# Softmax row factors of an attention stage: another instruction for the row sums, and Pool for two of the products

## The chip, the core and the metric

The program runs on one core of a Trainium2 chip. Five engines each work through their own queue in the order in which the program was written: TensorE (PE in the profile, with its weight loads as PEld), VectorE (DVE), ScalarE (ACT), GpSimd (POOL) and SyncE (SP), which here starts the DMA transfers. They meet at semaphores. The metric is the time of one execution in microseconds (us) on the device; lower is better.

## The reference

Three layers stand one behind the other. The change lies in the first, an attention over 2 batches, 8 heads, 576 tokens and head size 64; what the two expert layers behind it compute is only named here.

```python
scores = scale * np.matmul(q_rot, k_rot.transpose(0, 1, 3, 2))
scores = scores - np.max(scores, axis=-1, keepdims=True)
attn = np.exp(scores)
attn = attn / (np.sum(attn, axis=-1, keepdims=True) + 1e-09)
attn_out = np.matmul(attn, v)
...
x = _moe_ref(x=x, **moe_kwargs)             # 4 experts, all of them for every token
return _moe2_ref(x=x, **moe2_kwargs)        # 8 experts, one for each token
```

## The kernel before

**Tiles.** The 16 heads are worked off as 8 pairs. For pair `i` the scores of 2 x 576 rows are made in nine chunks of 128 rows by 576 columns: chunks 0 to 3 are rows of the first head, 5 to 8 of the second, and chunk 4 holds the last 64 rows of both. All products keep single precision by splitting each operand into a high and a low part (`..._hi` on one engine, the difference `..._lo` on another).

**One pair.** `load` brings q and k by DMA, `rope` turns them (three operations over 1152 columns, on Pool for nearly all pairs), `split_hi` (ACT) and `split_lo` (L187, Pool) write the parts to tile `n`, of which there is one, and `spread` (L224) copies `n` by ten DMAs of SP's queue to the operands `ka`, `kb`, `qa`, `qb`. Then for each chunk PE makes the scores (`qk`, L327, tile `sc`, a ring of two), DVE takes the negated row maximum (`row_max`, L337, tile `nm`), and ACT the exponential with its row sum (`exp`, L344), which lands in a column of tile `sum`. PE turns the exponentials round (`pt`, L382 to L389), ACT and DVE split them (`pt_hi` L407, `pt_lo` L411), PE multiplies by v (`av`, L424), ACT and DVE bring the halves together in `t` (L432, L438).

**The row factors.** When all nine chunks of a pair have their sums, DVE adds 1e-9 (`row_sum`, L350, `rs`), takes the reciprocal (`row_factor`, L354), and spreads it in two ways: `rest_factor` (L359) multiplies the block mask `blk` (128 x 128) by the factor of chunk 4 and gives `mrs`, and `wide_factor` (L365) repeats the other eight factors 64 times each and gives `rb` (128 x 512). The table `ENG` has `wide_factor` on Pool for seven pairs and on DVE for pair 1. A round later `rmat` on PE turns `rb` round with four transposes (L444) and multiplies `mrs` by `id2`, two identities above each other (L446); `x_norm` (DVE, L455) multiplies `t` by the result, and `x_hi`, `x_lo` write the input of the next layer.

**What sets the order.** `plan` hands every operation to a list scheduler with a rank (`POS`, a table of numbers), an engine, a planned cost and the operations it depends on. The scheduler (`Schedule.run`) plays the plan through and writes the instructions in the order that comes out. On the chip each engine then keeps to that order and waits wherever it comes too early. So `rmat`, `x_norm` and the products by v of pair `i` lie between the scores of pair `i+1`.

**Memory.** The tiles of the pairs' inputs lie in pools on the right side of the SBUF, among them `at_qf`. When the last scores are made, these are closed and the weights of the first expert (`load1`, L648, units `raw0` to `raw3`) are loaded over them. In the first expert layer PE multiplies without a gap (L784 to L786, then L800 to L802).

Of the kernel before, what the change touches and what calls it, by code (L numbers as in the profile page):

```python
# [10 lines left out]
F32 = mybir.dt.float32  # L11
# [84 lines left out]
class Attention:  # L96
# [40 lines left out]
    }  # L137

    ENG = {("rope", 0): "gggggggg", ("rope", 1): "gggggggg", ("rope", 2): "vvgggggg", ("split", 0): "aaaaaaaa",
           ("split", 1): "gggggggg", ("v", 0): "aaagaaaa", ("v", 1): "gggggggg", ("wide", 0): "gvgggggg",  # L140
           ("x", 0): "aaaagggg", ("x", 1): "gggggggg", ("rope1q", 0): "ggv", ("rope1k", 0): "vvv",
           ("split1", 0): "avav", ("first", 0): "vvgvvvvgvgvvgvvg", ("w_lo", 0): "gggv"}
    ENGINES = {"a": "ACT", "v": "DVE", "g": "POOL"}
# [1 line left out]
    def __init__(self, tc, ctx, tails, cst, qk, v, cs, xh, xl):  # L145
        self.tc, self.nc, self.cst = tc, tc.nc, cst
        self.qk_d, self.v_d, self.xh, self.xl = qk, v, xh, xl
        pool = lambda n, b, **k: ctx.enter_context(tc.tile_pool(name=n, bufs=b, **k))
        self.p_x = tails.enter_context(tc.tile_pool(name="at_x", bufs=2))
        self.p_vs = pool("at_vs", 3)  # L150
        self.p_e = pool("at_e", 13)
        self.p_sm = pool("at_sm", 2)
        self.early = ExitStack()
        pool_r = lambda n, b: self.early.enter_context(tc.tile_pool(name=n, bufs=b, side="right"))
        self.p_raw = pool_r("at_raw", 2)
        self.p_n = pool_r("at_n", 1)
        self.p_k = pool_r("at_k", 2)
        self.ps_sc = pool("ps_sc", 2, space=PSUM)
        self.first = ExitStack()
        self.ps_first = self.first.enter_context(tc.tile_pool(name="ps_first", bufs=2, space=PSUM))  # L160
        self.ps_pt, self.pool = None, pool
        nc = self.nc
        fixed = pool("at_fix", 1)
        self.pth = fixed.tile([128, 2, 4, S], F32R, name="pth")
        self.ptl = fixed.tile([128, 2, 4, S], F32R, name="ptl")
        self.p4 = fixed.tile([128, 2, S], F32R, name="p4")
        fixed = pool_r("at_qf", 1)
        self.rope_t, self.cs_d = fixed.tile([128, 2, 2, S], F32, name="cos_sin"), cs
        self.qa = [fixed.tile([128, 640], F32R, name=f"qa{j}") for j in range(2)]
        self.qb = [fixed.tile([128, 640], F32R, name=f"qb{j}") for j in range(2)]  # L170
        for j in range(2):
            nc.vector.memset(self.qa[j][:, S:640].bitcast(F32), 0.0)
            nc.vector.memset(self.qb[j][:, 512:S].bitcast(F32), 0.0)
        self.st = [dict() for _ in range(NPAIR)]

    def by(self, eng):
# [155 lines left out]
    def row_max(self, i, c):  # L332
        nc, st = self.nc, self.st[i]
        if "nm" not in st:
            st["nm"] = self.p_sm.tile([128, 9], F32, name="nm")
            st["sum"] = self.p_sm.tile([128, 9], F32, name="sum")
        nc.vector.tensor_reduce(out=st["nm"][:, c:c + 1], in_=st["sc", c][:, :, :SH],  # L337
                                axis=AX.XY, op=ALU.max, negate=True)

    def exp(self, i, c):  # L340
        nc, st = self.nc, self.st[i]
        e = st["e", c] = self.p_e.tile([128, S], F32, name="e")
        col = 8 if c == 4 else (2 * c if c < 4 else 2 * (c - 5) + 1)
        nc.scalar.activation(out=e.rearrange("p (a b) -> p a b", a=2), in_=st.pop(("sc", c))[:, :, :SH],  # L344
                             func=AF.Exp, bias=st["nm"][:, c:c + 1], accum_out=st["sum"][:, col:col + 1])

    def row_sum(self, i):
        nc, st = self.nc, self.st[i]
        rs = st["rs"] = self.p_sm.tile([128, 9], F32, name="rs")
        nc.vector.tensor_scalar(out=rs, in0=st["sum"], scalar1=1e-9, scalar2=None, op0=ALU.add)  # L350

    def row_factor(self, i):
        rs = self.st[i]["rs"]
# [1 line left out]

    def rest_factor(self, i):
        nc, st = self.nc, self.st[i]
        mrs = st["mrs"] = self.p_sm.tile([128, 128], F32, name="mrs")
        nc.vector.tensor_scalar(out=mrs, in0=self.cst["blk"], scalar1=st["rs"][:, 8:9], scalar2=None, op0=ALU.mult)  # L359

    def wide_factor(self, eng, i):
        st = self.st[i]
        rb = st["rb"] = self.p_sm.tile([128, 8, 64], F32, name="rb")
        sh = [128, 8, 64]
        self.by(eng).tensor_tensor(out=rb, in0=self.cst["one"].unsqueeze(2).to_broadcast(sh),  # L365
                                in1=st["rs"][:, 0:8].unsqueeze(2).to_broadcast(sh), op=ALU.mult)

    def pt(self, i, u):
        nc, st = self.nc, self.st[i]
# [70 lines left out]
    def rmat(self, i):  # L440
        nc, st = self.nc, self.st[i]
        ps = self.ps_sc.tile([128, 2, 512], F32, name="sc").rearrange("p a b -> p (a b)")
        for c in range(4):
            nc.tensor.transpose(ps[:, c * 128:(c + 1) * 128],  # L444
                                st["rb"][:, 2 * c:2 * c + 2].rearrange("p a b -> p (a b)"), self.cst["ident"])
        nc.tensor.matmul(ps[:, 512:S], st["mrs"], self.cst["id2"], start=True, stop=True)  # L446
        st["r"] = ps[:, 0:S]

    def x_parts(self, i):
# [29 lines left out]
    def plan(self, last_round):  # L479
# [15 lines left out]
        for i in range(NPAIR):  # L495
# [36 lines left out]
            for c in range(9):  # L532
# [8 lines left out]
            e = [D["exp", i, c] for c in range(9)]  # L541
            f = op("row_factor", i, 0, "DVE", 9, self.row_sum, i, after=e)
            f = op("row_factor", i, 1, "DVE", 60, self.row_factor, i, after=[f])
            f = [op("row_factor", i, 2, "DVE", 128, self.rest_factor, i, after=[f]),
                 op("row_factor", i, 3, self.letter("wide", 0, i), 400, self.wide_factor, self.letter("wide", 0, i), i,
                    after=[f])]

            def av(p, *keys):
                return [D["av", p, 5 * j + k] for j, k in keys if p >= 0]
# [909 lines left out]
```

## Time and profile before

| | us |
|---|---|
| three timed runs | 791.31, 791.35, 791.45 |
| median | 791.35 |
| the profiled execution | 791.62 |
| its span, first to last instruction | 789.4 |
| mean granted clock of TensorE | 0.993 |

The median and the profiled execution differ by 0.27 us, and 2.22 us of the execution lie outside the span. Over the whole span PE is busy for 94%, DVE for 60%, ACT for 49%, Pool for 18%. The stages differ much: the attention fills the first 184 us, the first expert layer the middle, the routed layer the end.

Times in the rows further down are us from the start of the span. A row of the timeline gives the start, the duration, the engine, the line of the program, the operation with the tiles that it writes and reads, and in square brackets how long the engine had been idle before and what ended that.

### The profile page before, as it was taken

The numbers are of one execution on the slowest core, as the hardware profiler recorded it, in microseconds if no ns is written. First come the engines' busy times: TensorE is split into PE (matmuls) and PEld (weight loads), VectorE is DVE, ScalarE is ACT, GpSimd is POOL, SyncE is SP. The second block draws the span as 40 slices with busy tenths as digits, with TensorE's granted clock in tenths as the row PEclk, the third lists the DMA queues.
The fourth block names the chain that finished last, engine by engine and source line by source line (L and its number), as shares of the span: only waits on it lengthen the run. The fifth ranks groups of instructions, "written<-read, shape, count | busy, mean of one in ns | idle before, by whom it ended". The sixth has DMA issues, their size and how long they took to land. (4 is left out here: it accounts for less than half of the span.)

```text
span 789.4 us, 11018 instructions
## 1 busy us (share of the span) xinstructions
PE 743.1 (94%) x4002; PEld 651.9 (83%) x4002; DVE 471.2 (60%) x876; ACT 390.2 (49%) x793; POOL 145.3 (18%) x118
## 2 busy tenths in 40 slices
PE   1798988899999999999999999999998999999997
PEld 1687877798998999999899899999986678888885
DVE  7988999998222252213522124322367999999993
ACT  4687888786101232111320113211224899999993
POOL 4767785324100000000000000000032001000000
PEclk9899999999999999999999999999999999999999
DMA  5766664615360069910282000000043266594010
GB/s 196 208 167 189 169 167 90 146 65 212 113 199 1 1 208 271 324 51 1 66 265 97 1 1 0 1 1 1 1 187 147 80 236 232 206 365 177 27 42 17
DMA packets 31836, 97.26 MB, mean 123 GB/s; under 512 B 4638, under 2 KB 6174, under 8 KB 25760
## 3 DMA queue, kind: packets, MB, share of 16 engines
q1 hardware_dynamic: 29936, 91.77, 37.2%
q0 software_dynamic: 1840, 4.73, 1.6%
q8 instruction: 33, 0.54, 0.3%
q14 instruction: 27, 0.22, 0.1%
HBM read 58.32 MB, written 27.09 MB: 108 GB/s over the span
## 5 line engine op out<-in xcount | busy, mean ns | idle before, releaser
L790 DVE SCALAR_TENSOR_TENSOR hl<-ps,hh 128x384 fp32r<-128x384 f32 x96 | 53.5, 558 | 269.6 <-ACT hh L789 269.6
L789 ACT ACTIVATE hh<-ps 128x384 fp32r<-128x384 f32 x96 | 47.2, 492 | 304.3 <-PE ps L786 302.7
L654 DVE TENSOR_TENSOR wl<-raw,wh 128x512 fp32r<-128x512 f32 x284 | 178.6, 687 | 7.0 <-ACT wh L653 7.0
L653 ACT ACTIVATE wh<-raw 128x512 fp32r<-128x512 f32 x284 | 156.6, 627 | 4.1 <-SPq L1238 2.5
L784 PE MATMUL ps<-xh,wh 128*128 128x384 f32 x384 | 130.1, 339 | 0.0
L786 PE MATMUL ps<-xh,wl 128*128 128x384 f32 x384 | 129.5, 337 | 0.0
L785 PE MATMUL ps<-xl,wh 128*128 128x384 f32 x384 | 129.3, 337 | 0.0
L800 PE MATMUL acc<-wh,hh 128*128 128x512 f32 x288 | 114.2, 397 | 0.0
L802 PE MATMUL acc<-wh,hl 128*128 128x512 f32 x288 | 114.1, 396 | 0.0
L801 PE MATMUL acc<-wl,hh 128*128 128x512 f32 x288 | 113.5, 394 | 0.0
L785 PEld LDWEIGHTS ps<-xl,wh 128*128 128x128 f32 x384 | 72.1, 188 | 3.9
L784 PEld LDWEIGHTS ps<-xh,wh 128*128 128x128 f32 x384 | 72.1, 188 | 3.9
L786 PEld LDWEIGHTS ps<-xh,wl 128*128 128x128 f32 x384 | 72.0, 188 | 0.0
L901 POOL TENSOR_TENSOR ss<-ss,half 128x1 f32<-128x1 f32 (+1 forms) x5 | 3.5, 705 | 364.3 <-DVE sq L890 364.2
L802 PEld LDWEIGHTS acc<-wh,hl 128*128 128x128 f32 x288 | 54.1, 188 | 12.6
L800 PEld LDWEIGHTS acc<-wh,hh 128*128 128x128 f32 x288 | 54.1, 188 | 9.1 <-issue 0.8
L801 PEld LDWEIGHTS acc<-wl,hh 128*128 128x128 f32 x288 | 54.1, 188 | 8.8
L344 ACT ACTIVATE e<-sc,nm 128x576 f32<-128x576 f32 x72 | 53.4, 743 | 8.6 <-DVE nm L337 8.3
L337 DVE TENSOR_REDUCE nm<-sc 128x1 f32<-128x576 f32 x72 | 53.8, 750 | 3.1 <-PE sc L327 2.0
L389 PE MATMUL pt<-ident,e 128*128 128x128 f32 (+1 forms) x304 | 47.9, 283 | 6.1 <-DVE ptl L411 5.5
L327 PE MATMUL sc<-ka,qa 128*128 128x288 f32 x160 | 33.9, 333 | 17.0 <-POOL qa L187 14.7
L411 DVE TENSOR_TENSOR ptl<-pt,pth 128x512 fp32r<-128x512 f32 x68 | 45.7, 680 | 2.2 <-ACT pth L407 1.4
(231 smaller groups left out, 1240.5 us busy)
## 6 DMA issues: line engine op xcount, KB each, us to landing
raw<-in_w_dram SPq DMA_DIRECT2D x40, 1024.0 KB, 5.8
xs<-z SPq DMA_DIRECT2D x10, 2056.0 KB, 14.1
raw<-in_qk_dram SPq DMA_DIRECT2D x7, 1152.0 KB, 5.4
ka<-n SPq DMA_DIRECT2D x14, 288.0 KB, 3.9
kb<-n SPq DMA_DIRECT2D x14, 288.0 KB, 4.6
xin<-xs SPq DMA_DIRECT2D x13, 257.0 KB, 4.0
rv<-in_v_dram SPq DMA_DIRECT2D x8, 320.0 KB, 5.4
qa<-n SPq DMA_DIRECT2D x14, 144.0 KB, 4.2
```

The source lines that it names most:

```text
L337: nc.vector.tensor_reduce(out=st["nm"][:, c:c + 1], in_=st["sc", c][:, :, :SH], axis=AX.XY, op=ALU.max, negate=True)
L344: nc.scalar.activation(out=e.rearrange("p (a b) -> p a b", a=2), in_=st.pop(("sc", c))[:, :, :SH], func=AF.Exp, bias=st["nm"][:, c:c + 1], ...
L389: nc.tensor.transpose(ps[0:n, c * 128:(c + 1) * 128], st["e", c + 5 * h][:, k * 128:k * 128 + n], ident)
L653: nc.scalar.activation(out=hi, in_=raw, func=AF.Copy)
L654: nc.vector.tensor_tensor(out=lo, in0=raw, in1=hi.bitcast(F32), op=ALU.subtract)
L784: nc.tensor.matmul(o, wcut(self.wh[u], k), xh[:, k, cs], start=(k == 0), stop=False)
L785: nc.tensor.matmul(o, wcut(self.wh[u], k), xl[:, k, cs], start=False, stop=False)
L786: nc.tensor.matmul(o, wcut(self.wl[u], k), xh[:, k, cs], start=False, stop=(k == 3))
L790: nc.vector.scalar_tensor_tensor(out=hl, in0=o, scalar=0.0, in1=hh.bitcast(F32), op0=ALU.max, op1=ALU.subtract)
L800: nc.tensor.matmul(acc, hh[:, js], wh, start=(f == 0), stop=False)
L801: nc.tensor.matmul(acc, hh[:, js], wl, start=False, stop=False)
L802: nc.tensor.matmul(acc, hl[:, js], wh, start=False, stop=(f == 7))
```

## The change

The row sums get a fixed tile for even and one for odd pairs, `sums[i % 2]`, with two columns for every chunk: the sum is written to the first, and the second holds 1e-9 from the start, set once by DVE. `row_sum` adds the two columns with `tensor_reduce` instead of adding a constant with `tensor_scalar`. `rest_factor` multiplies `id2` (128 x 64) by the factor, on Pool instead of DVE, and `rmat` exchanges the operands: `blk` is now the stationary one and `mrs`, half as wide, the moving one. `wide_factor` stands on Pool for all eight pairs. In the plan `rest_factor` gets Pool and 64 columns.

```diff
     ENG = {("rope", 0): "gggggggg", ("rope", 1): "gggggggg", ("rope", 2): "vvgggggg", ("split", 0): "aaaaaaaa",
-           ("split", 1): "gggggggg", ("v", 0): "aaagaaaa", ("v", 1): "gggggggg", ("wide", 0): "gvgggggg",
+           ("split", 1): "gggggggg", ("v", 0): "aaagaaaa", ("v", 1): "gggggggg",
...
+        self.sums = [fixed.tile([128, 9, 2], F32, name=f"sum{j}") for j in range(2)]
+        for t in self.sums:
+            nc.vector.memset(t[:, :, 1], 1e-9)
...
-            st["sum"] = self.p_sm.tile([128, 9], F32, name="sum")
+            st["sum"] = self.sums[i % 2]
...
-                             func=AF.Exp, bias=st["nm"][:, c:c + 1], accum_out=st["sum"][:, col:col + 1])
+                             func=AF.Exp, bias=st["nm"][:, c:c + 1], accum_out=st["sum"][:, col, 0:1])
...
-        nc.vector.tensor_scalar(out=rs, in0=st["sum"], scalar1=1e-9, scalar2=None, op0=ALU.add)
+        nc.vector.tensor_reduce(out=rs, in_=st["sum"], axis=AX.X, op=ALU.add)
...
-        mrs = st["mrs"] = self.p_sm.tile([128, 128], F32, name="mrs")
-        nc.vector.tensor_scalar(out=mrs, in0=self.cst["blk"], scalar1=st["rs"][:, 8:9], scalar2=None, op0=ALU.mult)
-
-    def wide_factor(self, eng, i):
+        mrs = st["mrs"] = self.p_sm.tile([128, 64], F32, name="mrs")
+        nc.gpsimd.tensor_tensor(out=mrs, in0=self.cst["id2"], in1=st["rs"][:, 8:9].to_broadcast([128, 64]),
+                                op=ALU.mult)
+
+    def wide_factor(self, i):
...
-        self.by(eng).tensor_tensor(out=rb, in0=self.cst["one"].unsqueeze(2).to_broadcast(sh),
-                                in1=st["rs"][:, 0:8].unsqueeze(2).to_broadcast(sh), op=ALU.mult)
+        self.nc.gpsimd.tensor_tensor(out=rb, in0=self.cst["one"].unsqueeze(2).to_broadcast(sh),
+                                     in1=st["rs"][:, 0:8].unsqueeze(2).to_broadcast(sh), op=ALU.mult)
...
-        nc.tensor.matmul(ps[:, 512:S], st["mrs"], self.cst["id2"], start=True, stop=True)
+        nc.tensor.matmul(ps[:, 512:S], self.cst["blk"], st["mrs"], start=True, stop=True)
...
-            f = [op("row_factor", i, 2, "DVE", 128, self.rest_factor, i, after=[f]),
-                 op("row_factor", i, 3, self.letter("wide", 0, i), 400, self.wide_factor, self.letter("wide", 0, i), i,
-                    after=[f])]
+            f = [op("row_factor", i, 2, "POOL", 64, self.rest_factor, i, after=[f]),
+                 op("row_factor", i, 3, "POOL", 400, self.wide_factor, i, after=[f])]
```

The order of ACT's and SP's instructions stays as it was; PE's and DVE's changes by one exchange late in pair 7 beside what the diff itself takes out and puts in.

DVE in the middle of a round, about the normalisation of pair 2; before (`nm` is a row maximum, `ptl` and `p_132` low parts of turned exponentials, `t` the output of a pair):

```order
L438 TENSOR_TENSOR t<-av_843,t 64x288
L337 TENSOR_REDUCE nm<-sc 128x1
L411 TENSOR_TENSOR ptl<-pt,pth 128x512 x2
L337 TENSOR_REDUCE nm<-sc 128x1
L359 TENSOR_SCALAR mrs<-blk,rs 128x128
L411 TENSOR_TENSOR ptl<-pt,pth 128x512
L455 TENSOR_TENSOR t<-t,sc 128x576
```

The same place after the change:

```order
L443 TENSOR_TENSOR t<-av_842,t 64x288
L341 TENSOR_REDUCE nm<-sc 128x1
L416 TENSOR_TENSOR ptl<-pt,pth 128x512 x2
L341 TENSOR_REDUCE nm<-sc 128x1
L416 TENSOR_TENSOR ptl<-pt,pth 128x512
L460 TENSOR_TENSOR t<-t,sc 128x576
```

Only the multiplication of `mrs` is gone from DVE's queue.

Pool between the low parts of pair 3 and those of pair 4 (the two rows of `n`); the rows `raw` turn pairs 4 and 5, and `xl` is of pair 0. Before:

```order
L187 TENSOR_TENSOR n<-raw,n 128x1152
L203 TENSOR_TENSOR raw<-raw,cos_sin 128x1152 x2
L187 TENSOR_TENSOR xl<-t,xh 128x576
L205 TENSOR_TENSOR raw<-raw 128x1152
L203 TENSOR_TENSOR raw<-raw,cos_sin 128x1152
L187 TENSOR_TENSOR n<-raw,n 128x1152
```

After:

```order
L191 TENSOR_TENSOR n<-raw,n 128x1152
L370 TENSOR_TENSOR rb<-one,rs 128x512
L207 TENSOR_TENSOR raw<-raw,cos_sin 128x1152
L363 TENSOR_TENSOR mrs<-id_74,rs 128x64
L207 TENSOR_TENSOR raw<-raw,cos_sin 128x1152
L191 TENSOR_TENSOR xl<-t,xh 128x576
L209 TENSOR_TENSOR raw<-raw 128x1152
L207 TENSOR_TENSOR raw<-raw,cos_sin 128x1152
L191 TENSOR_TENSOR n<-raw,n 128x1152
```

`rb` and `mrs` of pair 1 have come in, ahead of the rows that turn pair 4; in the other rounds one `mrs` comes in. Near the end of the attention three first splits of weights (`wl`) have moved ahead of the low parts of pair 6's output (`xl`).

SP's queue where the weights of the first expert are loaded, with the semaphores that each transfer waits for; before:

```order
L765 DMA itau<-in_tau_dram 128x1 [waits DMAHW6_49]
L765 DMA tokid<-in_tokid_dram 128x9 [waits DMAHW7_49]
L648 DMA raw_2067<-in_w_dram 128x2048 [waits DMAHW1_49,DMAHW2_49,DMAHW0_49,PE_49]
L648 DMA raw_2068<-in_w_dram 128x2048
L648 DMA raw_2069<-in_w_dram 128x2048
```

After:

```order
L769 DMA itau<-in_tau_dram 128x1 [waits DMAHW6_49]
L769 DMA tokid<-in_tokid_dram 128x9 [waits DMAHW7_49]
L652 DMA raw_2063<-in_w_dram 128x2048 [waits DMAHW1_49,DMAHW0_49,DMAHW2_49,DVE_49,PE_49]
L652 DMA raw_2064<-in_w_dram 128x2048 [waits DVE_49]
L652 DMA raw_2065<-in_w_dram 128x2048
```

The order is the same, but the fixed sum tiles were put in the pool `at_qf`, over which these weights are loaded: units 1 and 2 now wait for DVE as well, namely for `row_sum` of pair 6 and of pair 7.

## Rows read from the trace of the kernel before

**Rows 1.** Page, the span in 40 slices: busy tenths of DVE

```profile
DVE  7988999998222252213522124322367999999993
```

**Rows 2.** Stretches: length; busy us of PE, PEld, DVE, ACT, Pool; clock, DMA

```profile
64.00:68.00 4.00, 4.00 (x21) 3.88 (x20) 2.36 (x5) 2.12 (x6) 3.01 (x2) 0.57 0.99 213
115.33:135.46 20.13, 17.85 (x129) 15.72 (x128) 19.45 (x30) 16.86 (x38) 12.70 (x7) 1.00 0.42 89
...
157.21:175.52 18.31, 18.13 (x139) 16.95 (x138) 17.11 (x32) 16.11 (x37) 3.13 (x3) 1.00 0.07 20
183.78:789.40 605.62, 593.78 (x2988) 518.32 (x2986) 303.66 (x604) 248.81 (x484) 36.57 (x52) 1.00 0.33 112
```

**Rows 3.** By stage, instructions on rs alone: DVE busy, Pool busy, clock, DMA

```profile
30.00:57.00 27.00, 2.08 (x3) 1.04 (x1) 0.93 0.72 177
57.00:76.00 19.00, 3.23 (x4) 0.00 (x0) 0.91 0.80 232
76.00:94.96 18.96, 2.48 (x3) 1.04 (x1) 1.00 0.60 148
94.96:115.33 20.37, 3.94 (x3) 1.04 (x1) 1.00 0.68 187
115.33:135.46 20.13, 3.70 (x3) 1.04 (x1) 1.00 0.42 89
135.46:156.00 20.54, 3.71 (x3) 1.04 (x1) 1.00 0.59 140
156.00:183.78 27.78, 1.87 (x6) 2.08 (x2) 1.00 0.29 114
```

**Rows 4.** Instructions on tile rs: count, ns shortest/median/longest, first and last start

```profile
L350 DVE TENSOR_SCALAR rs<-sum x8: 164/757/2015, 37.0 to 175.5; 128x9 f32<-128x9 f32 x8
L354 DVE RECIPROCAL rs<-rs x8: 215/216/217, 37.7 to 175.7; 128x9 f32<-128x9 f32 x8
L359 DVE TENSOR_SCALAR mrs<-blk,rs x8: 277/1308/1712, 38.0 to 178.8; 128x128 f32<-128x128 f32 x8
```

**Rows 5.** Timeline of DVE: the row sums of pair 4

```profile
117.27 2.01 DVE L350 TENSOR_SCALAR rs<-sum 128x9 f32<-128x9 f32 x1 [0.23 <-ACT e L344]
```

**Rows 6.** Timeline of Pool: split of pairs 3, 6; turn of pair 5

```profile
58.72 2.65 POOL L187 TENSOR_TENSOR n<-raw,n 128x1152 fp32r<-128x1152 f32 x1 [2.46 <-ACT n L182]
...
76.14 2.68 POOL L203 TENSOR_TENSOR raw<-raw,cos_sin 128x1152 f32<-128x1152 f32 x1 [2.01 <-DMA raw<-in_qk_dram]
...
116.59 2.65 POOL L187 TENSOR_TENSOR n<-raw,n 128x1152 fp32r<-128x1152 f32 x1 [0.41 <-ACT n L182]
```

**Rows 7.** Timeline of SP's queue: start and time of issuing alone

```profile
61.40 1.34 SPq L224 DMA_DIRECT2D ka<-n  x2
...
70.79 0.58 SPq L191 DMA_DIRECT2D raw<-in_qk_dram  x1
...
86.75 4.01 SPq L224 DMA_DIRECT2D qb<-n  x4
...
173.18 31.73 SPq L648 DMA_DIRECT2D raw<-in_w_dram  x7
```

**Rows 8.** Timeline of ACT: split of pair 5, first weight splits

```profile
94.96 1.18 ACT L182 ACTIVATE n<-raw 128x1152 fp32r<-128x1152 f32 x1
...
186.45 2.18 ACT L653 ACTIVATE wh<-raw 128x512 fp32r<-128x512 f32 x4
```

**Rows 9.** Timeline of PE: waits in pairs 0 and 1

```profile
39.90 0.40 PE L424 MATMUL av<-p,vs 128*128 128x288 f32 x1 [1.58 <-DVE p L411]
...
62.58 0.65 PE L389 MATMUL pt<-ident,e 128*128 128x128 f32 x4 [1.18 <-DVE ptl L411]
```

**Rows 10.** DMA issues, 0 to 200 us: KB each, median us to landing

```profile
raw<-in_w_dram SPq DMA_DIRECT2D x7, 1024.0 KB, 5.0
...
qb<-n SPq DMA_DIRECT2D x14, 16.0 KB, 2.0
```

**Rows 11.** Group of Pool by form, 0 to 250 us: busy us, mean ns

```profile
L850 POOL TENSOR_TENSOR scale<-scale,itau 128x8 f32<-128x8 f32 x1 | 0.2, 203 | 0.1
```

## The prediction

> **What bounds the kernel now.** I read the page's slices first, then the stretches, then what the changed instructions cost by stage. The slices [rows 1] show DVE nearly full in the first nine or ten of 40, the attention, and far from full in the middle. From 183.78 us on PE is busy for 593.78 of 605.62 us [rows 2]: the expert layers are PE's, no edited line runs there, and they move as a block with the moment at which the attention ends. So the change is worth what the end of the attention moves.
>
> Inside it one pair takes about 20 us. In the round from 115.33 to 135.46 DVE is busy for 19.45 of 20.13 us, PE for 17.85, ACT for 16.86, Pool for 12.70 [rows 2]. DVE sets the pace, and part of its busy time is no work. `row_sum` handles nine numbers a row and takes between 164 and 2015 ns, `mrs` between 277 and 1712 [rows 4]. In pair 4 `row_sum` starts at 117.27 and ends at 119.28 [rows 5]; Pool's subtraction for `n` started at 116.59 and ends at 119.24 [rows 6]. The nine numbers are held until Pool is through. The reciprocal, on the same engine and operand, takes 215 to 217 ns in all eight pairs [rows 4].
>
> Beside this. The Trainium skill (SBUF — State Buffer, "Who interferes with whom") says why: `tensor_scalar` can use the port pair that VectorE shares with GpSimd and is then blocked for the whole of the other's instruction, while `tensor_reduce` on trn2 never contends. The 2.01 us agree; a `tensor_reduce` from SBUF under a running Pool instruction is in no row here. By that rule the low end below is right; without it the third rival's 8 x 0.6 us would be lost.
>
> **The change part by part.** *What leaves DVE.* Rows 3 give the time of everything that touches `rs`, stage by stage. The stages are cut where ACT begins the high parts of `n` of the next pair, for a reason that follows. What stays of a pair is a row sum and a reciprocal. I take the row sum at 0.16, the shortest it is now, since the new form reads 18 numbers instead of nine; its bounds are that and the present mean of about 1.0 (median 0.76), if the reduction is held in the same way [rows 4]. I take the low end because the reciprocal, also SBUF to SBUF with one tensor input, never varies. With 0.22 for the reciprocal 0.38 stays, and the stages lose: 1.70 (to 57), 2.85 (to 76, with the wide factor of pair 1), 2.10, 3.56, 3.32, 3.33, and 1.11 (two pairs to the end). Together 17.97 us.
>
> *What comes to Pool.* Eight `mrs` of 128x64 and one `rb`. The `rb` costs 1.04 [rows 3]. An `mrs` lies between 0.20, a product of 128x8 [rows 11], and that 1.04; on a straight line between 8 and 512 columns it is an estimate of 0.3. So Pool gets 0.3 us more a round, up to 1.04, and has 7 idle in the round of rows 2. The result is wanted a whole round later (the `mrs` of pair 4 falls due behind 135), in pair 7 a few us later; PE's new wait for it costs nothing, and the `pt` and `av` queued behind it on PE aren't held.
>
> *What is neutral.* On Pool the first weight splits now stand ahead of pair 6's `xl`, which the expert layer reads only from its second block of tokens on, after eight groups of products. The product of `rmat` keeps 64 moving columns and a 128x128 stationary operand. The two fills with 1e-9 fall into DVE's first idle time. The sum column has another stride, which ACT writes as one number a row. On SP units 1 and 2 of the weights get a wait for `row_sum` of pairs 6 and 7. The last row sum starts at 175.5 [rows 4], the loads at 173.18 [rows 7]: unit 2, unit 3 behind it, and the next expert's loads come some 2.5 us later. A load lands 5.0 us after issue [rows 10], so unit 2 is there by about 181.5; ACT's first weight splits of that layer start at 186.45 [rows 8]. That cover is 5 us; without it the cost would be those 2.5.
>
> *How much reaches the end.* Stage by stage:
> - To 57 us: PE waits 1.58 for DVE's `p` of pair 0, right behind its `mrs` [rows 9]. Take 1.6.
> - To 76: with `rb` gone, PE loses its wait of 1.18 for `ptl` [rows 9]. After this gap PE ran from 64 to 68 at a granted clock of 0.57, a mix of the two levels 2.4 and 1.2 GHz [rows 2]; at full clock these 4.00 us would be 2.28. Without the gap I expect no fall: 1.18 + 1.72 = 2.9, about what DVE loses.
> - To 94.96: 2.1. Sum so far 6.6.
> - Here something else is late. Tile `n` exists once, and ACT can write pair 5's high parts at 94.96 [rows 8] only when the ten copies of pair 4 have landed. Going back: the last of them is issued by 90.76 [rows 7], lands 2.0 after an issue of 0.6 [rows 10], thus at 92.2. These copies follow Pool's split of pair 4, which follows the turn that started at 76.14 after waiting for its load [rows 6]; that load was issued at 70.79, behind the ten copies of pair 3 from 61.40 [rows 7], and those behind Pool's split at 58.72 [rows 6]. None of it has DVE in it. The chain moves only with its head, by the 1.6 of the first stage, so ACT can begin at 92.2 - 1.6 = 90.6 at the earliest: 4.4 instead of 6.6. ACT's queue is in order and the pair's last exponentials stand behind; all engines come to wait.
> - To 115.33 and to 135.46: 3.56 and 3.32 on offer. In the stretch from 157.21 to 175.52, in which nothing is held by Pool, PE does 139 instructions in 18.31 us; the 129 of a round would take 17.0 at that rate, 3.1 less than 20.13 [rows 2]. But ACT has 16.86 to do in such a round. I take 85%: 3.0 and 2.8.
> - To 156: ACT has no split of `n` left to do; 90% of 3.33: 3.0.
> - To the end: 80% of 1.11: 0.9.
>
> The sum is 4.4 + 3.0 + 2.8 + 3.0 + 0.9 = 14.1 us. From the profiled execution's 791.62 that gives 777.5. The median of the runs is 0.27 lower, so I forecast **777.3**.
>
> **The rivals.**
> *The loop over n doesn't hold* (copies land earlier, or the head moves more). Then the 6.6 stay, and the later stages give 85 to 100% of their 11.3: 16.2 to 17.9, thus 775.1 to 773.4. For it: the 2.0 us to landing are the median of 14 copies, not the last one's own time. Against: the order on Pool and SP is unchanged.
> *PE and ACT take over.* With DVE at 16.8 us a round, three engines with 16 to 17 us of work meet through rings of two; if 60% comes through behind the loop, 4.4 + 0.6 x 11.3 = 11.2, and 10 if PE's clock falls in the new hold at 90: 780 to 781.5. For it: ACT's 16.86. Against: the clean stretch.
> *The work comes back as waits.* If DVE waits for each Pool instruction that was added, 8 x 0.3 + 1.04 = 3.4 are lost, and if the new row sum is held like the old, another 8 x 0.6, the distance of the median from 0.16: gain 5.9 to 10.7, 780.6 to 785.4. The Trainium skill (Perfetto Trace Analysis, "Optimizing Scalar/DVE Operations") warns of just that: offloading between the two engines that share a read port might not help. Against it: DVE's remaining work in these rounds is `nm`, `ptl`, `p`, `t`, all with an operand in PSUM; their time isn't stretched while Pool is busy for 12.70 us of a round.
> *Slower: the clock.* If PE, waiting now for the loop in bursts, falls to the low level as from 64 to 68, a round whose work fills 17 us takes 34. One such round costs 17 and eats the 14.1; from about 0.8 of a round on the kernel is slower, with one and a half it is at 791.4 - 14.1 + 25.5 = 802.8. For it: a gap of 1.18 us was enough once. Against it: PE waits less than before, and the clock is 1.00 in every stage from 76 on [rows 3].
>
> **How the numbers follow.** Forecast 0.60; no loop 0.12; PE and ACT take over 0.16; work comes back 0.07; slower 0.03; no difference, some cover missing by the whole gain, 0.02. The bounds of the forecast itself (60 to 100% of what the rounds offer) are 11 to 16 us. The range takes in the first three cases and the better half of the fourth: 773.5 to 782.5. A measurement of this kernel can tell 0.2%, 1.6 us, from no change: faster 0.95, same 0.02, slower 0.03.
>
> **What would show it.** After the change `row_sum` should take one length in all pairs, near 0.17 us, and no product with `blk` or `one` stand on DVE. The rounds should be near 17 us with ACT and PE as full as DVE; ACT should wait near 90 us, in front of the high parts of pair 5, for something that is not DVE; PE's clock between 60 and 70 should be full. PE's first product of the expert layer should come near 169.7 instead of 183.78, and the 605.6 us behind it stay. The forecast is wrong if `row_sum` still varies with Pool, if a long wait of PE stands in front of `rmat`, or if the expert layer starts early and then waits for weights.

## The result, and the profile after

| | before | after |
|---|---|---|
| median of the runs (us) | 791.40 | 780.49 |
| the profiled execution | 791.62 | 780.67 |
| its span | 789.4 | 779.0 |

The ratio is 0.9858, with a 95% interval of 0.9841 to 0.9875. The kernel is faster by 10.9 us; 777.3 had been forecast, so 3.2 us of the forecast didn't come. Of all runs in this document one, 794.78 us of `part_sum`, was in the slow state; the ratios are those of the fast runs, and need not be the quotient of the two medians beside them. Line numbers after the change are four or five higher for the lines that follow the new ones.

First the page of the changed kernel, busy tenths in 40 slices of DVE, and the granted clock (9 is 90% or more); they answer to [rows 1].

```profile
DVE  7989899985212351222522225231467999999993
...
PEclk9899999999999999999999999999999999999999
```

The slices hardly differ: DVE stays nearly full in the attention, which is now shorter. What changed is seen in the stretches. A row gives the stretch, its length, the busy us of PE, PEld, DVE, ACT and POOL, the granted clock, the DMA share and GB/s; it answers to [rows 2, 3].

```profile
64.00:68.00 4.00, 3.73 (x29) 3.25 (x28) 3.87 (x8) 3.47 (x9) 4.00 (x3) 1.00 1.00 219
...
90.25:108.70 18.45, 16.43 (x114) 15.45 (x113) 14.94 (x26) 16.86 (x38) 14.69 (x8) 0.91 0.88 252
108.70:126.28 17.58, 17.12 (x129) 15.78 (x128) 16.52 (x29) 16.74 (x38) 14.70 (x8) 1.00 0.50 109
126.28:145.49 19.21, 18.75 (x142) 17.22 (x140) 18.16 (x32) 17.56 (x40) 7.59 (x6) 1.00 0.61 150
...
173.20:779.00 605.80, 593.76 (x2986) 518.41 (x2986) 301.89 (x602) 248.43 (x483) 34.55 (x51) 1.00 0.33 112
```

The undisturbed round from 108.70 takes 17.58 us instead of 20.13, and PE, with 17.12, is now the fullest engine in it, in front of ACT and DVE. The block of the expert layers is 605.80 long, against 605.62.

The instructions on tile `rs`, with count, ns shortest/median/longest, and first and last start in us, answer to [rows 4].

```profile
L354 DVE TENSOR_REDUCE rs<-sum x8: 163/173/174, 36.7 to 163.8; 128x9 f32<-128x18 f32 x8
L358 DVE RECIPROCAL rs<-rs x8: 215/216/216, 36.9 to 164.0; 128x9 f32<-128x9 f32 x8
L370 POOL TENSOR_TENSOR rb<-one,rs x8: 1033/1041/1054, 37.5 to 164.3; 128x512 f32<-128x512 f32 x8
L363 POOL TENSOR_TENSOR mrs<-id,rs x8: 289/298/321, 38.5 to 165.3; 128x64 f32<-128x64 f32 x8
```

The row sum takes one length in all pairs. At 36.71 it ran while Pool was turning (34.84 to 37.50), and at 128.22 while Pool worked on `n` (127.55 to 130.22), for 0.17 us each time.

Last the timeline of ACT, PE and again PE at two places (start, us, in brackets the idle time before and what ended it); they answer to [rows 8, 9].

```profile
90.25 1.16 ACT L186 ACTIVATE n<-raw 128x1152 fp32r<-128x1152 f32 x1 [1.88 <-DMA qb<-n]
...
92.19 0.80 PE L331 MATMUL sc<-ka,qa 128*128 128x288 f32 x4 [1.63 <-ACT e L348]
...
173.20 0.41 PE L788 MATMUL ps<-xh,wh 128*128 128x384 f32 x1 [1.87 <-DVE t L460]
```

The first two are the loop over `n`. The third is new: PE waits in front of the expert layer, where before it went straight on:

```profile
183.78 0.34 PE L784 MATMUL ps<-xh,wh 128*128 128x384 f32 x1
```

The high parts of pair 6 begin at 108.70 (before: 115.33), those of pair 7 at 126.28 (135.46), the row sum of pair 6 at 145.49 (157.21). So the gain of the span splits up like this:

| stretch | forecast | before | after | gain |
|---|---|---|---|---|
| to the high parts of pair 5 | 4.4 | 94.96 | 90.25 | 4.71 |
| from there to those of pair 6 | 3.0 | 20.37 | 18.45 | 1.92 |
| to those of pair 7 | 2.8 | 20.13 | 17.58 | 2.55 |
| to the row sum of pair 6 | 3.0 | 21.75 | 19.21 | 2.54 |
| to the first expert product | 0.9 | 26.57 | 27.71 | -1.14 |
| expert layers | 0 | 605.62 | 605.80 | -0.18 |
| sum | 14.1 | | | 10.40 |

The time outside the span is 0.55 shorter, which makes the 10.95 between the two profiled executions.

### The profile page after: what moved, and what is told of

Its sections match the earlier page's. It is cut to its first block, busy times and chain, and to the rows that moved or that the text cites. A ratio compares the mean times of both kernels' runs of the same rounds, so it can differ in the third digit from the quotient of the medians.

```text
span 779.0 us, 11020 instructions
## 1 busy us (share of the span) xinstructions
PE 739.0 (95%) x4002; PEld 651.3 (84%) x4002; DVE 455.4 (58%) x869; ACT 389.8 (50%) x793; POOL 146.7 (19%) x127
## 6 DMA issues: line engine op xcount, KB each, us to landing
xs<-z SPq DMA_DIRECT2D x10, 2056.0 KB, 14.1
```

## The experiments

The theory: DVE's freed time reaches the end stage by stage, capped once by the loop over `n`; what is missing went to three places, the new wait at 173.20, a low clock behind the hold at 90, and rounds that PE now sets. Rivals are named with each run. The kernels ran on three chips, so each is compared by its ratio to runs of the kernel before on its own chip; one table holds them all.

| run | median | before there | ratio, 95% interval |
|---|---|---|---|
| part_sum | 787.56 | 792.10 | 0.9926, 0.9904 to 0.9949 |
| part_small | 787.52 | 792.10 | 0.9942, 0.9925 to 0.9958 |
| part_wide | 792.95 | 792.10 | 1.0006, 0.9996 to 1.0017 |
| after_bank | 778.79 | 792.10 | 0.9831, 0.9819 to 0.9844 |
| undo_sum | 788.87 | 791.60 | 0.9970, 0.9960 to 0.9980 |
| after_n5 | 777.69 | 791.60 | 0.9829, 0.9817 to 0.9842 |
| after_both | 776.99 | 791.60 | 0.9816, 0.9803 to 0.9828 |
| part_wide_bank | 790.15 | 791.60 | 0.9984, 0.9975 to 0.9992 |
| after_again | 781.52 | 791.93 | 0.9873, 0.9858 to 0.9888 |
| after_twice | 781.27 | 791.93 | 0.9873, 0.9858 to 0.9888 |
| undo_small | 785.64 | 791.93 | 0.9922, 0.9908 to 0.9935 |
| after_all | 776.09 | 791.93 | 0.9809, 0.9796 to 0.9823 |

### Each part alone

**part_sum**: the kernel before, with the row sums alone changed.

```diff
-        nc.vector.tensor_scalar(out=rs, in0=st["sum"], scalar1=1e-9, scalar2=None, op0=ALU.add)
+        nc.vector.tensor_reduce(out=rs, in_=st["sum"], axis=AX.X, op=ALU.add)
```

> The kernel before with only the row sums changed: fixed sum tiles with 1e-9 beside each sum, added up by a tensor_reduce. Products for mrs and the wide factor of pair 1 stay on DVE. Theory A (DVE's time is what counts, stage by stage): row_sum of 8 pairs goes from some 8.0 us in total to 8 x 0.17, so 6.7 us leave DVE; at 85% some 5.5 us reach the end: 785 to 787. In this kernel rmat of pair 7 keeps its two PSUM banks, so the first product of the expert layer should not wait for x_norm of pair 7 on DVE. Theory B (the hold only moves: mrs, still on DVE, will be held by Pool instead of row_sum): mrs grows, under 3 us reach the end: 788.5 to 791. Theory C (DVE is full either way, each part alone brings nearly the whole gain of 10.9): 780 to 783.

The ratio says 5.9 us, with an interval of 4.0 to 7.6, since its runs scatter most. The trace shows both sides of it. First the instructions on tile `rs`:

```profile
L353 DVE TENSOR_REDUCE rs<-sum x8: 163/173/175, 36.9 to 172.1; 128x9 f32<-128x18 f32 x8
L362 DVE TENSOR_SCALAR mrs<-blk,rs x8: 277/746/4581, 37.3 to 175.3; 128x128 f32<-128x128 f32 x8
```

The timeline of DVE, of Pool and of PE around the longest `mrs`:

```profile
83.23 4.58 DVE L362 TENSOR_SCALAR mrs<-blk,rs 128x128 f32<-128x128 f32 x1
...
80.93 2.71 POOL L206 TENSOR_TENSOR raw<-raw,cos_sin 128x1152 f32<-128x1152 f32 x1
83.56 1.60 POOL L190 TENSOR_TENSOR vs<-rv,vs 128x640 fp32r<-128x640 f32 x1
85.09 2.64 POOL L208 TENSOR_TENSOR raw<-raw 128x1152 f32<-128x1152 f32 x1
...
88.47 1.06 PE L392 MATMUL pt<-ident,e 128*64 128x128 f32 x4 [3.50 <-DVE ptl L414]
```

The stretches: the round of this `mrs`, two of its us, and a round without a hold:

```profile
74.40:97.67 23.27, 19.47 (x129) 18.22 (x128) 20.91 (x30) 16.83 (x40) 14.47 (x7) 0.85 0.54 142
90.00:92.00 2.00, 2.00 (x11) 1.98 (x10) 1.44 (x2) 0.83 (x2) 1.28 (x1) 0.50 0.62 142
...
116.07:133.66 17.59, 17.15 (x129) 15.82 (x128) 16.74 (x30) 16.73 (x39) 14.49 (x7) 1.00 0.50 110
```

The row sum is free of Pool. In one round, though, `mrs`, still on DVE, is held through three Pool instructions in a row, from 83.23 until 87.81, a moment after Pool's last one ended at 87.73. PE then waits 3.50 for `ptl` and runs at the low level of its clock, 0.50 from 88 to 94. What theory B names happened in this round, what theory A names in the full round from 116.07, which takes 17.59. The eight `mrs` take 9.9 us in all here, 8.7 before. The gain is theory A's, 5.5 us; theory B's, under 3, lies outside the interval, and so does theory C's 10.9.

**part_small**: the kernel before, with `mrs` alone moved to Pool.

```diff
-        nc.vector.tensor_scalar(out=mrs, in0=self.cst["blk"], scalar1=st["rs"][:, 8:9], scalar2=None, op0=ALU.mult)
+        nc.gpsimd.tensor_tensor(out=mrs, in0=self.cst["id2"], in1=st["rs"][:, 8:9].to_broadcast([128, 64]),
+                                op=ALU.mult)
```

> The kernel before with only the small factor changed: mrs of 128x64 on Pool, operands of the product in rmat exchanged. The row sum stays a tensor_scalar. Theory A: some 8.7 us of mrs leave DVE, at 85% 7.4; but here the ring of score tiles changes its step, and rmat of pair 7 stands in the banks where the expert layer's first product goes, so that this product waits some 1.9 us for x_norm of pair 7: 7.4 - 1.9 = 5.5, 785 to 787. Theory B (the held time moves to row_sum, which stays longer under Pool): row_sum's mean over 1.2 us, under 3 us reach the end: 788.5 to 791. Theory C (each part alone brings nearly the whole gain): 780 to 783.

By the ratio it gains 4.6 us. Three row sums are held long, for 2.01 to 2.50 us:

```profile
L350 DVE TENSOR_SCALAR rs<-sum x8: 163/512/2501, 37.1 to 170.2; 128x9 f32<-128x9 f32 x8
```

All eight together take 8.0 us, as many as before. PE's last row of products by v starts at 177.42, 6.2 us earlier than the 183.65 of before, and then waits 1.87 for `x_norm` as theory A said, whose 5.5 us come out within 1 us. B falls, as the row sums' mean is 1.0 us and not over 1.2, and so does C.

**part_wide** and **part_wide_bank**: the kernel before with the wide factor of pair 1 on Pool; the second also with the expert layer's PSUM tiles at the other end.

```diff
-           ("split", 1): "gggggggg", ("v", 0): "aaagaaaa", ("v", 1): "gggggggg", ("wide", 0): "gvgggggg",
+           ("split", 1): "gggggggg", ("v", 0): "aaagaaaa", ("v", 1): "gggggggg", ("wide", 0): "gggggggg",
...
-        self.ps_t = pool("ps_t", 2, space=PSUM)
+        self.ps_t = pool("ps_t", 2, space=PSUM, side="right")
```

> The kernel before with only the wide factor of pair 1 put on Pool. Theory A: 2.57 us leave DVE at 59.4; PE's wait of 1.18 at 62.58 and the fall of the clock from 64 to 68 (1.72 us) vanish, 2.9 us; the new wait for x_norm of pair 7 in front of the expert layer takes 1.9 back: 790 to 791. Theory B (the fall of the clock has another cause and stays): 1.2 gained, 1.9 lost: 791.7 to 792.5, slower than before.

> The kernel before with the wide factor of pair 1 on Pool, and the expert layer's two PSUM tiles at the other end of the PSUM. Theory A (the part alone gained 1.8 us in the attention and lost 2.0 to the new wait in front of the expert layer): 1.6 us less than the part alone, ratio to before 0.998. Rival (the new wait costs nothing, the part alone is worth nothing): 1.000.

Alone, the part is worth nothing that can be measured; the time is the one that theory B had named. Its reason isn't: from 62 to 68 the clock is 1.00. The high parts of pair 4 begin at 73.70 instead of 76.05, the lead is 1.8 us at PE's last product by v (181.85 against 183.65), where 2.9 had been expected, and then the new wait takes it back. PE's first expert product in part_wide:

```profile
184.01 0.41 PE L784 MATMUL ps<-xh,wh 128*128 128x384 f32 x1 [1.87 <-DVE t L455]
```

And in part_wide_bank, where PE goes straight on:

```profile
182.97 0.39 PE L784 MATMUL ps<-xh,wh 128*128 128x384 f32 x1
```

With the tiles elsewhere the wait is gone and the ratio is 0.9984, as expected. The wait alone doesn't explain why part_wide gains nothing. Behind it PE's clock falls to its low level, and the expert layers take 607.29 us instead of 605.62; two us behind the wait, and the whole block, in part_wide:

```profile
186.01:188.01 2.00, 2.00 (x8) 2.00 (x7) 0.07 (x1) 0.60 (x2) 0.24 (x2) 0.50 0.84 356
184.01:791.30 607.29, 595.40 (x2986) 520.06 (x2986) 301.93 (x602) 248.36 (x483) 34.22 (x50) 1.00 0.33 112
```

Eight traces here have the wait of 1.87. In five the clock falls behind it and the block takes 607.20 to 607.31 (part_small, part_wide, undo_sum, undo_small, after_twice); in three it doesn't, and the block takes 605.60 to 605.80 (the changed kernel in both its traces, and after_n5). In the six traces without the wait the clock is 1.00 in the first 12 us of the block. So the wait costs some 1.5 us more in some executions. An edit that is only to free DVE had paid its gain back 100 us later, through the placing of a PSUM tile.

### Parts taken back

**undo_sum**: the changed kernel with the row sum as a `tensor_scalar` on nine numbers again. **undo_small**: the changed kernel with `mrs` back on DVE as before.

> The changed kernel with the row sum taken back to a tensor_scalar on nine numbers; both factors stay on Pool. Theory A: row_sum is held again by whatever Pool does, up to 2.0 us in each of four or five pairs, some 7 us in total; at 60 to 85% that is 4 to 6 us more than the changed kernel: 784.5 to 787, ratio to before 0.991 to 0.994. Rival: since the full rounds of the changed kernel are PE's (17.13 busy of 17.58) and DVE has 1 us of slack in them, only a part of the hold shows: under 2 us, 781 to 782.5.

> The changed kernel with mrs back on DVE as a tensor_scalar of 128x128; row sum and wide factor stay as changed. Theory A (what DVE is held costs nearly in full in the rounds that DVE paces): mrs takes 1.3 to 4.6 us in most pairs, 9 to 12 us in total, of which 6 to 9 reach the end: 786 to 789. Rival (the row sum was the worse of the two because it stands in front of the pair's factors, mrs is wanted only a round later): mrs is held, but only 2 to 4 us reach the end: 782 to 785.

undo_sum gives away 7.7 us or more (0.9970 against 0.9873 of the changed kernel in its second measurement), above the expected 4 to 6. In the traces 5.9 us of it lie in front of the expert layer (179.10 against 173.20) and 1.4 behind, where the clock falls after the wait. The timeline of DVE and Pool at one of the holds, and then two rounds:

```profile
113.33 1.94 DVE L354 TENSOR_SCALAR rs<-sum 128x9 f32<-128x9 f32 x1 [0.30 <-ACT e L348]
...
112.58 2.66 POOL L191 TENSOR_TENSOR n<-raw,n 128x1152 fp32r<-128x1152 f32 x1 [0.76 <-ACT n L186]
```

```profile
90.44:111.32 20.88, 17.87 (x114) 16.47 (x113) 16.59 (x26) 16.85 (x37) 16.91 (x9) 0.84 0.79 226
111.32:130.54 19.22, 17.36 (x129) 15.79 (x128) 18.16 (x29) 16.74 (x38) 12.64 (x8) 1.00 0.44 93
```

In the second round the row sum, 1.77 longer than 0.17, makes the round 1.64 longer (19.22 against 17.58), nearly in full: the rival, by which DVE's slack would hide it, falls. In the first, the wait for the copies (1.81 us on ACT) and a row sum held for 1.99 add up, the clock goes down to 0.50, and the round takes 20.88.

undo_small loses 3.9 us by the ratios, at the upper end of the rival's 2 to 4 and short of theory A's 6 to 9. Its profiled execution (790.70, the longest of six, the others 784.94 to 786.41) is another matter. Two of its `mrs`, Pool's instructions at both places, PE's wait behind the longer one, and two us behind that:

```profile
81.10 2.45 DVE L363 TENSOR_SCALAR mrs<-blk,rs 128x128 f32<-128x128 f32 x1
118.97 4.99 DVE L363 TENSOR_SCALAR mrs<-blk,rs 128x128 f32<-128x128 f32 x1
...
80.81 2.65 POOL L207 TENSOR_TENSOR raw<-raw,cos_sin 128x1152 f32<-128x1152 f32 x1
83.42 1.56 POOL L191 TENSOR_TENSOR vs<-rv,vs 128x640 fp32r<-128x640 f32 x1
...
117.10 2.68 POOL L207 TENSOR_TENSOR raw<-raw,cos_sin 128x1152 f32<-128x1152 f32 x1
119.75 1.56 POOL L191 TENSOR_TENSOR vs<-rv,vs 128x640 fp32r<-128x640 f32 x1
121.28 2.60 POOL L209 TENSOR_TENSOR raw<-raw 128x1152 f32<-128x1152 f32 x1
...
124.62 0.80 PE L393 MATMUL pt<-ident,e 128*64 128x128 f32 x4 [3.91 <-DVE ptl L415]
...
126.00:128.00 2.00, 2.00 (x11) 1.99 (x11) 1.46 (x3) 0.86 (x2) 1.40 (x1) 0.50 0.06 10
```

The first `mrs` got in when one Pool instruction ended, though the next followed at once. The second was held through three, and PE waited 3.91 for the `ptl` behind it and then ran at 0.50. In this execution the eight `mrs` take 13.8 us, and the first expert product comes 8.45 us later than in the changed kernel, which is near theory A's numbers. That this happens less in the other five is likely from their times, and not shown.

Alone the parts bring 5.9, 4.6 and -0.5 us, 10.0 in sum, and all three together 10.0 to 11.2 by the two measurements; the intervals are too wide to say more. Only undo_sum, with 2.4, stays below the 4.1 of the two parts that it keeps. Nor does the hold simply pass from one instruction to the other. The row sums take 8.0 us in all before and in part_small, 7.3 in undo_sum; `mrs` takes 8.7 before, and more where it is the one that is left: 9.9 in part_sum and 13.8 in this trace of undo_small, most of the growth in one long hold each.

### The three places of the missing gain

**after_bank**: the changed kernel with the second edit of part_wide_bank alone.

> The changed kernel, with the two PSUM tiles of the expert layer's products taken from the other end of the PSUM: they lie over the tiles of the products by v instead of over rmat of pair 7. Theory A (1.9 us of the missing gain are PE's wait for x_norm of pair 7): the first product of the expert layer starts at 171.3 to 171.9 instead of 173.20, the block behind it stays 605.8: 778.6 to 779.2. Rival D (the wait turns into one for the split weights or for hl a little later, PE being held by the ring of two there): first product earlier, block longer by as much: 780 to 780.8.

PE's first expert product, and the stretch from there to the end:

```profile
170.32 0.45 PE L788 MATMUL ps<-xh,wh 128*128 128x384 f32 x1 [0.27 <-DVE t L443]
```

```profile
170.32:776.10 605.78, 593.89 (x2986) 518.44 (x2986) 303.64 (x604) 248.43 (x484) 36.64 (x52) 1.00 0.33 112
```

From the start of the last product by v (169.75) to the first of the expert layer 0.57 us pass instead of 2.16 (171.04 to 173.20): 1.6 us, and the block behind keeps its length, so rival D falls. The remaining lead of this execution comes from a round that the next paragraphs explain.

**after_n5**: pair 5's split is written to the half of `xl` that is still unused, so it needn't wait for the copies out of `n`.

```diff
-            st["n"] = self.p_n.tile([128, 4, S], F32R, name="n")
+            st["n"] = self.xl[:, :, S:] if i == 5 else self.p_n.tile([128, 4, S], F32R, name="n")
```

> The changed kernel with the split of pair 5 written to the still unused half of xl instead of the single tile n. Theory A (the loop over n holds all engines near 90): ACT begins the high parts of pair 5 at some 88.4 instead of 90.25 without a wait for the copies, PE's wait behind it (1.63 at 92.19) vanishes, and so does the low clock behind it where it occurred: the end of the attention comes 1.9 to 2.7 us earlier, 777.8 to 778.6. Rival (something else holds ACT or PE at the same place, the load of pair 6 or the operands of pair 5): under 0.5 us, 780 to 780.5.

ACT at the split of pair 5, and the stretch of the round:

```profile
87.31 1.18 ACT L186 ACTIVATE xl<-raw 128x1152 fp32r<-128x1152 f32 x1
```

```profile
88.20:106.00 17.80, 17.37 (x130) 15.90 (x128) 16.73 (x30) 16.93 (x39) 14.83 (x8) 1.00 0.92 265
```

ACT begins without a wait, PE's wait behind it is gone, and the clock is 1.00. Executions start up to 0.9 us apart (the high parts of pair 2 begin at 39.41 here, at 40.32 in the changed kernel), so the distance from pair 4's high parts to pair 6's is the safer number: 35.10 us instead of 37.98. That is 2.9 us for the loop and the clock behind it.

**after_again**: the changed kernel a second time.

> The changed kernel itself once more, on the chip of the runs beside it, to see what of its trace comes and goes. Expected: ratio to before 0.985 to 0.987; ACT waits 1.8 to 1.9 us for the copies of pair 4 near 90 and PE 1.87 in front of the expert layer, as in the first trace. If the low clock behind the hold (0.54 and 0.61 from 94 to 98 in the first trace) belongs to every execution, the stage from pair 5's high parts to pair 6's takes 18.4 to 18.5 again; if it comes and goes, 17.6.

The stage from pair 5's high parts to pair 6's takes 18.35 us, much as in the first trace (18.45), while in after_bank, whose program is the same up to 170 us, it takes 17.59. Two us of this stage in after_again:

```profile
94.00:96.00 2.00, 2.00 (x11) 2.00 (x10) 1.75 (x4) 1.33 (x4) 2.00 (x2) 0.50 0.54 111
```

And the whole stage in after_bank:

```profile
89.81:107.40 17.59, 15.55 (x115) 14.17 (x114) 14.85 (x26) 16.74 (x38) 14.73 (x8) 1.00 0.88 243
```

So the low clock comes and goes: it is in two of the three traces, and costs 0.8 us where it is. ACT had waited 1.88 and 1.89 us for the copies there, and 1.74 in after_bank, where the clock stayed. The ratio, 0.9873, is just above the expected 0.985 to 0.987; the profiled execution (780.20) is the fastest of four, and what the others (781.49 to 781.99) lost isn't shown.

**after_both** and **after_all**: both edits; in after_all the fixed sum tiles also stand in the pool of `pth` and `ptl` (left side), so that no weight load waits for a row sum.

> Both: pair 5's split in xl, and the expert layer's two PSUM tiles at the other end of the PSUM. Theory A (two separate losses): the gains add, 1.9 to 2.7 and 1.6: 776.0 to 777.2, ratio to before near 0.981. Rival (the second hides the first, because weights and splits of the expert layer aren't ready that early): 777.5 to 778.6, with a new wait of PE in the first expert products.

> The changed kernel with pair 5's split in xl, the expert layer's PSUM tiles at the other end, and the fixed sum tiles in the pool of pth and ptl, so that the loads of weight units 1 and 2 don't wait for the row sums of pairs 6 and 7. Theory A (that wait is covered): the same as with the first two alone, 776.0 to 777.5, ratio near 0.9815, no PE wait for weights in either. Rival (the later weights cost something in the first expert layer): 1 to 2.5 us less, 774 to 776.

The two losses are separate: 0.9816 with both, against 0.9831 and 0.9829 with one each; since the intervals overlap, the traces must carry it. In after_both the distance between the high parts is 35.10 again and the first expert product comes 0.58 behind the last product by v. after_all has the lowest ratio here, 0.9809 (776.09 us), though not clear of after_both; its block of the expert layers is 605.81 long, and PE's list of waits up to 190 us names no weights, so the waits of the loads for the row sums had indeed cost nothing. Two of its stretches, a round and the expert layers:

```profile
105.58:123.15 17.57, 17.12 (x129) 15.78 (x128) 16.50 (x29) 16.74 (x38) 15.57 (x9) 1.00 0.55 128
168.49:774.30 605.81, 593.86 (x2986) 518.45 (x2986) 303.56 (x604) 248.57 (x484) 36.78 (x52) 1.00 0.33 112
```

**after_twice**: the changed kernel, each factor made twice on Pool.

> The changed kernel with both factors made twice on Pool (the same product written a second time): 1.34 us more for Pool in each pair, 10.7 in total. Theory A (Pool's new work is covered, Pool having 2.9 us idle in a round of 17.58): within 0.6 us of the changed kernel beside it. Rival (Pool is close to setting the pace by way of the turns and splits): 2 to 10 us slower than the changed kernel.

One of its rounds, POOL's 15.96 being the fifth of the busy times:

```profile
107.64:125.33 17.69, 17.24 (x130) 15.91 (x129) 16.62 (x29) 16.83 (x38) 15.96 (x10) 1.00 0.55 130
```

It takes 781.27 us beside 781.52: Pool's work is covered, and would be at twice its size. In its trace the first expert product comes at 172.24, against 172.71 in after_again, and the block behind takes 1.47 us longer:

```profile
172.24:779.50 607.26, 595.54 (x2986) 519.97 (x2986) 301.86 (x602) 248.26 (x483) 34.63 (x51) 0.99 0.33 112
```

The clock is 0.56 in the first two us of this block and 0.59 in the next two, as in the other traces in which it falls behind the wait, so the longer block is no sign of Pool's added work.

## Why the prediction was right where it was, and where it failed

**The hold of the row sum: right.** The low end, 0.16, was taken for it, and 0.163 to 0.174 came in all pairs. The reciprocal's constant 0.22 had been the right row to judge by. The Trainium skill (SBUF — State Buffer, "Who interferes with whom") had said that `tensor_reduce` never contends with GpSimd; the trace agrees, with 0.17 us under a running Pool instruction.

**Pool's new work: right.** An `mrs` takes 0.30, as interpolated, and after_twice shows that it costs nothing. The third rival, work that comes back as waits, falls with that, and so does, for this change, the warning of the Trainium skill (Perfetto Trace Analysis, "Optimizing Scalar/DVE Operations") that offloading between the two engines might not help. The runs differ: part_small, with the move of `mrs` from DVE to Pool alone, takes 4.6 us less.

**The first stages and the loop over n: right.** The low clock of 64 to 68 [rows 2] is gone, the two early stages gave 5.3 us (76.05 to 70.72) instead of 4.5, of which some tenths can be the start of the execution, and the loop then capped the lead. ACT had been expected to begin pair 5's high parts at 90.6 at the earliest; it began at 90.25 after a wait of 1.88 for the copies. after_n5 shows that the loop is what held it.

**The rounds: right in kind, 0.7 us too large.** The step took 85% and 90% of what DVE loses; 2.55 of 3.32 (77%) and 2.54 of 3.33 (76%) came. What PE needs had been read off another stretch, as 17.0 us a round, and 85% made a round of 17.3 out of that. But 17.12 us of a round are PE's, and a round without a hold takes 17.57 to 17.69 in after, after_bank, after_twice, after_all and part_sum alike. That PE sets this length is read from its busy time; no run takes work from PE. Here the second rival was right: PE has taken over the pace, but at 17.58 and not at the 18.1 that its 60% would mean.

**The round behind the hold: 1.1 us too large.** Only 1.92 of 3.0 came. The forecast had left the fall of the clock to the second rival, which says "10 if PE's clock falls in the new hold at 90". That is what happened; by after_bank's round, 0.86 of the 1.1 are the clock's.

**The end: the step that failed.** "80% of 1.11: 0.9" counted DVE's time alone; -1.14 came. Leaving out the new wait of 1.87 the gain would have been 0.73. The wait was not in the sum, and not in a rival. Its cause can be followed in the program: the score tiles are a ring of two pairs of PSUM banks, and which of them `rmat` of pair 7 gets depends on which of the two was given back first. With a factor on Pool the sequence shifts once in pair 1, behind `rmat` of pair 0, and `rmat` of pair 7 ends up in the banks over which the expert layer's first tile `ps` is laid. PE must then wait until `x_norm` of pair 7 has read it, and that in turn waits for the last products by v. part_sum, the only part in which no such shift occurs, doesn't have the wait; part_small and part_wide have it; after_bank and part_wide_bank, which only move the tile, lose it. The prediction looked at the order of PE's instructions, which is nearly the same, and at the waits on SP; where a tile lies had changed under the order. The waits of PE's first expert product in the changed program, among which there now was one for DVE, would have told it. Behind this wait the clock can fall, which costs some 1.5 us more; it did not in this trace, and the prediction had looked for a fall of the clock in the rounds only.

**The sum.** Of 14.1 us 10.4 came: 0.3 more up to the loop, 1.1 less behind it, 0.7 less in the next two rounds, 2.0 less at the end, 0.2 in the expert layers. The time came out where the second rival had put it, 780 to 781.5, but only about half of the shortfall is by its mechanism. That the stated range holds the time is in part luck: the 2.0 us at the end belong to no case from which it was made.

## What to carry to other kernels

A `tensor_scalar` on tiny SBUF operands can be the dearest instruction of a round when Pool is busy. Where only one of two such instructions is changed, look at the other: here the row sums that were left took as long as before, the `mrs` that were left longer. When an edit changes which engine gives a tile back, compare the waits and the places of the buffers on every engine down to the next stage, not the order of the instructions only; a gain can be lost at a tile that the edit never names, and a wait there can cost more than its length when the clock falls behind it. And when an engine's share of a round is freed, see how full the next engine will be: in the new round of 17.58 us PE is busy for 17.12, so by these rows what else might leave DVE would gain at most half a us there, an estimate.

## What the runs showed of the hardware

A `tensor_scalar` of DVE that is held is mostly let in when the running Pool instruction ends, even if the next one follows without a gap: in undo_small the `mrs` from 81.10 ended at 83.55, Pool's instructions ended at 83.46 and began at 83.42. In the seven traces with such instructions on DVE 19 holds ended at a border of that kind. But it doesn't always get in: one waited through three Pool instructions in part_sum, 4.58 us, and one in undo_small, 4.99. Before, the longest hold had been 2.02. What decides which of the two happens is not shown. The Trainium skill (SBUF — State Buffer, "Who interferes with whom") has the second one blocked until the other's instruction is over; most holds agree, and in the two longest the wait went on until the row of Pool instructions was over.

TensorE's clock fell to its low level (0.50, 1.2 of 2.4 GHz) behind waits of PE of 3.50 and 3.91 us, behind the hold at 90 in two of three traces of the same program, and behind the wait of 1.87 in front of the expert layer in five of the eight traces that have it: such falls may be a part of the scatter between executions of one kernel. What decides whether one comes was not settled: ACT's wait in front of the hold at 90 differs by 0.15 us between the traces with and without it, and the wait of 1.87 is the same in all eight.
